# The prologue of an FFT filter and FFN kernel: zeta of batch 0 in one tile, an x load of batch 1 moved into a filter's buffer, and PSUM banks shared between two small stages

## The chip, the cores and the metric

The kernel runs on one core of one Trainium2 chip. The metric is device time in microseconds (us). A time is the median of several executions; the profile is one of them.

TensorE (PE) multiplies and writes to PSUM (eight banks). VectorE (DVE) and ScalarE (ACT) evict PSUM into SBUF. GpSimd (POOL) here only casts fp32 to fp16. SyncE (SP) issues nearly all DMA transfers, from one queue, in program order.

## The reference

```python
def _attn_ref(x, filt_r, filt_i):             # x: 8 x 3008 x 256
    X = np.fft.rfft(x, axis=1)
    Y = X * (filt_r + 1j * filt_i)[None]
    return np.fft.irfft(Y, n=x.shape[1], axis=1)

def _moe_ref(x, w_in, w_out):                 # 24064 tokens, 256 -> 2048 -> 256
    h = np.maximum(x @ w_in, 0.0)
    return h * h @ w_out
```

## The kernel before

The FFT is done by matmuls. The FFN of all 24064 tokens is the bulk of PE's work, and the transforms of batches 1 to 7 are slipped between its matmuls. Only batch 0 has nothing to hide behind: until its filtered signal is there, no FFN matmul can start. That prologue takes about 54 us, and the change concerns it alone. Its steps are: `chunk_a0` (first transform, giving uT), `turn_u` (uT turned by matmuls with the identity), `place_f` (the filter put in order by matmuls with the 0/1 matrix sPF, result sF), `unit_b` (second transform, and the product with sF on DVE), `unit_p0` (first half of the way back, giving zeta, stored to DRAM as dZ), `read_z` (dZ read back in another layout), `unit_y` (psY, the last half), and then `ffn_g1`. Batch 1's first transform (`chunk_a(1, c)`, psA) stands on PE between the last `unit_p0` and the first `unit_y`.

```python
p_x32 = pool(bufs=2)      # x in fp32, then w_in in fp32
p_ze  = pool(bufs=3)      # zeta
p_y   = pool(bufs=2)      # tag "yt": the two filters in fp32, then products, then yt
p_h2  = pool(bufs=2)      # tag "h2": several early tiles, then h of the FFN
...
def bank_pair(name):                 # rotates through the 8 PSUM banks, two at a time
    k = npair[0] % 4; npair[0] += 1
    if k < 2: t = psH(name); return [t[:, 0, :], t[:, 1, :]], [(t, 0)]
    ...                              # k == 2: two psF banks, k == 3: two psO banks
...
def unit_p0(k):
    ze = p_ze.tile([128, 6, D], F16, tag="ze", name=f"ze_0_{k}")
    ps = psH(f"psP_0_{k}")
    ...                                                           # 8 matmuls
    nc.scalar.copy(out=ze[:, 0:4, :], in_=...ps...)
    nc.sync.dma_start(out=dZ[0]...[:, 4 * k:4 * k + 4, :], in_=ze[:, 0:4, :])
...
for k in range(2): load_win(k)            # w_in into the two x32 buffers
for c in (0, 2, 1, 3): chunk_a0(c)
...                                       # POOL: filter casts, then w_in casts
for k in range(6): turn_u(k)
nc.vector.tensor_copy(...)                # last quarter of the filter casts, on DVE
for k in range(4): place_f(0, k, nc.vector if k % 2 else nc.scalar)    # psH banks only
place_f(1, 0, nc.scalar)
load_wide(1, 0); cast_wide(1, 0, nc.gpsimd, nc.gpsimd)      # x of batch 1, first third
for k in range(7):
    if k < 6:
        unit_b(0, 2 * k)
        if k < 5: place_f(1, k + 1, nc.scalar)
        unit_b(0, 2 * k + 1)
    if k > 0: unit_p0(k - 1)
    if k < 2: place_f(0, k + 4, nc.scalar)
    if k in (2, 3): load_wide(1, k - 1); cast_wide(1, k - 1, nc.gpsimd, nc.gpsimd)
    if k == 5: read_z(0, 0, (0,))         # first half of the first zt: needs stores 0 to 2
read_z(0, 0, (1,)); read_z(0, 1)
for c in (0, 2, 1): chunk_a(1, c)         # psA
...
for n in range(4): unit_y(0, n)           # psY; the FFN follows
```

## Time and profile before

| | before |
|---|---|
| time, median | 801.57 us (3 runs), 801.13 us (4 runs, with one beside the changed kernel) |
| span of the profiled run (its time: 800.30 us) | 798.5 us |
| PE busy | 782.8 us, 98% |
| granted clock, mean of the span | 0.995 |
| first psY starts | 52.84 us |

The span is the profiled execution on the core. Since PE is busy nearly always after the prologue, everything after the first psY is nearly a block of fixed length: in the profiles of this case 745.2 to 747.7 us lie behind it. So what counts first is when that block starts; the 2.5 us by which its length differs come back below. The lines that show this, and the waits in front of it, are in the prediction.

### The profile page before, as it was taken

What the parts mean: (1) busy time and instruction counts of PE and PEld (TensorE: products, weight loads), DVE (VectorE), ACT (ScalarE), POOL (GpSimd) and SP (SyncE); (2) the same over time, 40 slices, a digit from 0 to 9 for tenths busy, and PEclk for the clock granted to TensorE, in tenths of its full rate; (3) what the DMA queues carried; (4) which work ended last, traced back from release to release, by engine and by line L of the source; (5) the groups of instructions that cost most, each with busy time, mean ns of one, the idle gap of its engine ahead of it and who ended that gap; (6) DMA issues with size and microseconds to landing.
All of it is one profiled execution on the core that took longest, in us unless ns stands there. A gap on an engine that the chain in (4) does not pass through costs nothing.

```text
span 798.5 us, 14777 instructions
## 1 busy us (share of the span) xinstructions
PE 782.8 (98%) x6102; PEld 553.3 (69%) x6102; DVE 552.7 (69%) x897; ACT 554.3 (69%) x705; POOL 18.5 (2%) x23
## 2 busy tenths in 40 slices
PE   8979999999999999999999999999999999999998
PEld 5746767667676676867778676776767667676666
DVE  7847995579855897559965699556995589553342
ACT  4756776767767676777776677676777767766663
POOL 3320000000000000000000000000000000000000
PEclk9989999999999999999999999999999999999999
DMA  9886455335723467055561565525563342511111
GB/s 362 317 272 209 123 149 138 98 128 158 200 65 106 149 164 189 27 152 157 129 177 55 166 157 131 136 66 160 148 181 92 88 142 81 123 45 41 40 41 53
DMA packets 88124, 108.10 MB, mean 135 GB/s; under 512 B 6273, under 2 KB 78849, under 8 KB 83585
## 3 DMA queue, kind: packets, MB, share of 16 engines
q1 hardware_dynamic: 87848, 106.98, 46.8%
q8 instruction: 48, 0.79, 0.4%
q10 hardware_dynamic: 144, 0.18, 0.1%
q14 instruction: 20, 0.16, 0.1%
q0 software_dynamic: 64, 0.00, 0.0%
HBM read 58.90 MB, written 48.23 MB: 134 GB/s over the span
## 4 chain that ended last, share of the span: by engine, by line
PE 90%; DMA 7%; ACT 1%; DVE 1%; SPq 0%; issue 0%; ACTq 0%
PE psO L566 40%; PE psH L551 39%; PE psY L521 3%; PE psA L349 3%; PE psB L436 3%; PE psP L485 2%; DMA sPF<-cPF 2%; DMA ut<-dU 2%; DMA dZ<-ze 2%; DMA zt<-dZ 1%; PE psf L283 1%; PE psf L286 1%; ACT h L555 1%; ACT sF L293 0%; ACT ze L473 0%; DVE yt L530 0%
## 5 line engine op out<-in xcount | busy, mean ns | idle before, releaser
L555 ACT ACTIVATE h<-psH 128x1024 f16<-128x1024 f32 x376 | 384.8, 1024 | 190.3 <-PE psH L551 188.3
L566 PE MATMUL psO<-sWout,h 128*128 128x256 f16 x3008 | 388.6, 272 | 0.0
L551 PE MATMUL psH<-yt,sWin 128*128 128x512 f16 (+7 forms) x1728 | 386.9, 351 | 1.2 <-ACT h L555 0.4
L566 PEld LDWEIGHTS <-h 128*128 128x128 f16 x3008 | 290.6, 98 | 77.3
L559 DVE TENSOR_TENSOR h<-h 128x1024 f16<-128x1024 f16 x376 | 253.9, 685 | 100.7 <-ACT h L555 99.2
L551 PEld LDWEIGHTS <-sWin 128*128 128x128 f16 x1728 | 159.4, 98 | 101.1 <-issue 2.6
L444 DVE TENSOR_TENSOR prod<-psB,sF 128x1024 f16<-128x1024 f32 x84 | 102.5, 1220 | 6.4 <-PE psB L436 6.1
L530 DVE CAST yt<-psY 128x376 f16<-128x376 f32 x62 | 33.9, 549 | 57.8 <-PE psY L521 57.8
L355 DVE CAST u<-psA 96x512 f16<-96x512 f32 x50 | 34.3, 687 | 46.8 <-PE psA L349 45.1
L487 ACT CAST ze<-psP 128x512 f16<-128x512 f32 x84 | 49.2, 585 | 17.9 <-PE psP L485 16.0
L573 ACT COPY ost<-psO 128x512 f32<-128x512 f32 x94 | 55.5, 590 | 7.2 <-PE psO L566 5.8
L521 PEld LDWEIGHTS <-zt 112*128 112x128 f16 x512 | 34.8, 98 | 13.2 <-issue 3.1
L521 PE MATMUL psY<-sC,zt 112*128 112x94 f16 x512 | 42.2, 205 | 1.4 <-DMA zt<-dZ 1.0
L458 DVE TENSOR_TENSOR yf<-prod,yf 128x512 f16<-128x512 f16 x84 | 35.7, 425 | 2.9
L436 PE MATMUL psB<-ut,sSB 128*128 128x256 f16 x192 | 36.5, 272 | 0.8 <-DMA ut<-dU 0.6
L349 PE MATMUL psA<-x,sC 94*96 94x512 f16 x96 | 36.6, 382 | 0.0
L436 PEld LDWEIGHTS <-sSB 128*128 128x128 f16 x192 | 18.6, 98 | 21.4 <-issue 2.3
L485 PE MATMUL psP<-yf,sSP 128*128 128x256 f16 x168 | 32.1, 273 | 0.2 <-ACT yt L528 0.2
L528 ACT CAST yt<-psY 128x376 f16<-128x376 f32 x66 | 30.8, 468 | 1.1 <-PE psY L521 1.0
L328 DVE CAST x<-x 94x2048 f16<-94x2048 f32 x24 | 29.2, 1216 | 0.0
L353 ACT CAST u<-psA 96x512 f16<-96x512 f32 x50 | 28.6, 572 | 0.0
L451 DVE COPY yf<-prod 64x512 f16<-64x512 f16 x84 | 24.3, 289 | 2.9
(61 smaller groups left out, 248.7 us busy)
## 6 DMA issues: line engine op xcount, KB each, us to landing
x<-in_x_dram SPq DMA_DIRECT2D x20, 768.0 KB
zt<-dZ SPq DMA_DIRECT2D x64, 192.0 KB
dU<-u SPq DMA_DIRECT2D x28, 384.0 KB
dZ<-ze SPq DMA_DIRECT2D x28, 384.0 KB
out_dram<-ost SPq DMA_DIRECT2D x32, 256.0 KB
out_dram<-ost SPq DMA_DIRECT2D x64, 128.0 KB
ut<-dU SPq DMA_DIRECT2D x7, 1024.0 KB
xw<-in_x_dram SPq DMA_DIRECT2D x6, 1024.0 KB
```

Source lines behind the costliest of these rows:

```text
L349: nc.tensor.matmul(ps[0:96, :], sSA, x16s[(b, c)][:, m, :], start=True, stop=True)
L436: nc.tensor.matmul(ps[:, i * D:(i + 1) * D], sSB[:, 2 * p + i, :], uts[b][:, 2 * p + i, :], start=True, stop=True)
L444: nc.vector.tensor_mul(out=prod, in0=ps.rearrange("p (a d) -> p a d", d=D).unsqueeze(1).to_broadcast([128, 2, 2, D]), in1=sF[:, :, 2 * p:2 ...
L458: nc.vector.tensor_add(out=yf, in0=prod[:, 0], in1=yf)
L485: nc.tensor.matmul(ps[:, i * D:(i + 1) * D], sSP[:, 2 * p + i, :], yf[:, i, :], start=True, stop=True)
L487: nc.scalar.copy(out=zes[(b, c)][:, 2 * i6:2 * i6 + 2, :], in_=ps.rearrange("p (a d) -> p a d", d=D))
L521: nc.tensor.matmul(ps[:, 94 * jj:94 * jj + 94], zt[:, 4 * (g % 2) + jj, dt * 128:(dt + 1) * 128], sSY, start=True, stop=True)
L551: nc.tensor.matmul(ps[:, i, o:o + n], sWin[:, dt, jt * 128:(jt + 1) * 128], yts[b][:, dt, r:r + n], start=(dt == 0), stop=(dt == 1))
L555: nc.scalar.activation(out=h2[:, 2 * s:2 * s + 2, :], in_=ps, func=AF.Relu)
L559: nc.vector.tensor_mul(out=v, in0=v, in1=v)
L566: nc.tensor.matmul(pso[g][:, t % 2, :], h2s[g][:, jt, t * 128:(t + 1) * 128], sWout[:, jt, :], start=(jt == 0), stop=(jt == NJT - 1))
L573: nc.scalar.copy(out=ost, in_=pso[g])
```

## The change

The intent is threefold. First, zeta of batch 0 no longer rotates through three buffers but lies in one tile, so that its evictions wait for no store. Second, one x load of batch 1 goes into the buffer of the filter's real part as soon as that has been cast, ahead of the other two; load 1 is also issued one step sooner. Third, turning and placing are interleaved and rotate through all eight banks, and the last quarter of the filter casts goes from DVE to POOL.

```diff
-        pool = p_h2 if (b, k) == (0, 2) else p_x32
+        pool, tag = (p_x32, "x32") if k < 2 else (p_y, "yt") if b else (p_h2, "h2")
...
-    def place_f(im, k, eng):
-        t = psH(f"psf_{im}_{k}")
-        banks, groups = [t[:, 0, :], t[:, 1, :]], [(t, 0)]
+    def place_f(im, k, eng, rotate=False):
+        if rotate:
+            banks, groups = bank_pair(f"psf_{im}_{k}")
+        else: ...                                   # as before
...
     def unit_p0(k):
-        ze = p_ze.tile([128, 6, D], F16, tag="ze", name=f"ze_0_{k}")
+        if k == 0:
+            zes[0] = p_h2.tile([128, NC, D], F16, tag="h2", name="ze_0")
+        ze = zes[0][:, 4 * k:4 * k + 4, :]
...
-    for im, e in ((0, e0), (0, e1), (1, e0)):
+    for im, e in ((0, e0), (0, e1), (1, e0), (1, e1)):      # casts on POOL
...
+    load_wide(1, 2)
+    load_wide(1, 0)
+    for k in (2, 0):
+        cast_wide(1, k, nc.gpsimd, nc.gpsimd)
     for k in range(6):
-        turn_u(k)
-    nc.vector.tensor_copy(out=f16s[0][:, 1, e1], in_=f32s[1][:, e1])
-    for k in range(4):
-        place_f(0, k, nc.vector if k % 2 else nc.scalar)
+        turn_u(k, nc.vector if k in (1, 3, 4, 5) else nc.scalar)
+        if k > 2:
+            place_f(0, k - 3, nc.scalar, True)
+    place_f(0, 3, nc.vector, True)
     place_f(1, 0, nc.scalar)
-    load_wide(1, 0)
-    cast_wide(1, 0, nc.gpsimd, nc.gpsimd)
...
-        if k in (2, 3):
-            load_wide(1, k - 1)
-            cast_wide(1, k - 1, nc.gpsimd, nc.gpsimd)
+        if k == 1:
+            load_wide(1, 1)
+            cast_wide(1, 1, nc.gpsimd, nc.gpsimd)
```

More of the change, by code (lines that the diff above doesn't have):

```diff
@@ L217, in load_wide @@
         v1 = xrows[b * S + 2048:b * S + 3072, :].rearrange("(p m) d -> p m d", m=8)
-        pool = p_h2 if (b, k) == (0, 2) else p_x32
-        t = pool.tile([128, 8, D], F32, tag="h2" if pool is p_h2 else "x32", name=f"xw_{b}_{k}")
+        pool, tag = (p_x32, "x32") if k < 2 else (p_y, "yt") if b else (p_h2, "h2")
+        t = pool.tile([128, 8, D], F32, tag=tag, name=f"xw_{b}_{k}")
         nc.sync.dma_start(out=t, in_=(v0[:, 0:8, :], v1, v0[:, 8:16, :])[k])
@@ L269 @@
     f16s = []
-    def place_f(im, k, eng):
-        t = psH(f"psf_{im}_{k}")
-        banks, groups = [t[:, 0, :], t[:, 1, :]], [(t, 0)]
+    def place_f(im, k, eng, rotate=False):
+        if rotate:
+            banks, groups = bank_pair(f"psf_{im}_{k}")
+        else:
+            t = psH(f"psf_{im}_{k}")
+            banks, groups = [t[:, 0, :], t[:, 1, :]], [(t, 0)]
         for i in range(4):
@@ L402, in chunk_a0, with turn_u @@
                     nc.vector.tensor_copy(out=o, in_=pv)
-    def turn_u(k):
-        if k > 3:
-            npair[0] = k - 2
+    def turn_u(k, eng):
         banks, groups = bank_pair(f"psT_{k}")
@@ L412, in turn_u @@
                 nc.tensor.matmul(o, uT[:, dt, 4 * k + i, :], ident, start=True, stop=True)
-        eng = pair_engine()
         for t, i in groups:
@@ L472, in unit_p0 @@
                                  prod[:, v, i % 2, :], start=(v == 0), stop=(v == 1))
-        nc.scalar.copy(out=ze[:, 0:4, :], in_=ps.rearrange("p t (a d) -> p (t a) d", d=D))
+        nc.scalar.copy(out=ze, in_=ps.rearrange("p t (a d) -> p (t a) d", d=D))
         nc.sync.dma_start(
             out=dZ[0].rearrange("(s p) d -> p s d", p=128)[:, 4 * k:4 * k + 4, :],
-            in_=ze[:, 0:4, :])
+            in_=ze)
     def unit_p(b, p):
```

## The prediction

> **What bounds the kernel now.** I read the page first. TensorE (PE) is busy nearly throughout, so after the start-up the span is a fixed quantity of matmuls, and only the start can give time back.
>
> ```profile
> PE 782.8 (98%) x6102; PEld 553.3 (69%) x6102; DVE 552.7 (69%) x897; ACT 554.3 (69%) x705; POOL 18.5 (2%) x23
> ```
>
> Everything the diff touches lies in the first 65 us (batch 0's filter product, batch 1's first transform). So I read the chain of waits over that stretch (start us, length, what):
>
> ```profile
> 36.16 1.00 ACT ze L473
> 37.17 7.05 DMA dZ<-ze
> 44.32 1.02 ACT ze L473
> 45.36 4.06 DMA dZ<-ze
> 49.44 3.27 DMA zt<-dZ
> ```
>
> Zeta is evicted from PSUM by ScalarE (ACT) into `ze`, three buffers in rotation, stored to `dZ` and read back as `zt`. Eviction 5 needs the buffer of store 2, which was issued at 37.17 and landed only at 44.22. ACT stood still for it for 3.58 us. Then come the last store (4.06 us) and the read back (3.27 us), and only then psY, which feeds the FFN.
>
> Why did a 256 KB store take 7 us? The timeline of GpSimd (POOL) shows what else was in the queue: batch 1's x in three loads of 1 MB, cast in the order they landed.
>
> ```profile
> 31.67 2.02 POOL L310 CAST sWin<-win 128x1024 f16<-128x1024 f32 x2 [0.45 <-DMA win<-in_moe_w_in_dram]
> 36.62 2.02 POOL L227 CAST xw<-xw 128x1024 f16<-128x1024 f32 x2 [2.93 <-DMA xw<-in_x_dram]
> 43.58 2.02 POOL L227 CAST xw<-xw 128x1024 f16<-128x1024 f32 x2 [4.93 <-DMA xw<-in_x_dram]
> 46.77 2.02 POOL L227 CAST xw<-xw 128x1024 f16<-128x1024 f32 x2 [1.17 <-DMA xw<-in_x_dram]
> ```
>
> The loads reuse the buffers of w_in, so they cannot start before the POOL casts from 29.2 us on. PE waits for the second one, too, and pays twice. The windows below are 3.4 us long; columns are PE, weight load, DVE, ACT and POOL busy, granted clock, DMA share, GB/s:
>
> ```profile
> 29.20:32.70 3.50, 3.39 (x38) 2.95 (x36) 3.29 (x4) 3.24 (x4) 3.05 (x4) 1.00 0.40 89
> 39.50:42.90 3.40, 1.57 (x11) 0.93 (x10) 1.65 (x2) 1.01 (x1) 0.00 (x0) 0.99 0.97 295
> 42.90:46.30 3.40, 1.62 (x4) 0.77 (x4) 0.00 (x0) 1.16 (x2) 2.02 (x2) 0.50 1.02 367
> 46.30:49.70 3.40, 3.40 (x9) 1.62 (x8) 1.22 (x1) 1.57 (x3) 2.02 (x2) 0.50 0.52 164
> ```
>
> The DMA engines idle at 29 to 33 us (share 0.40), just before they become the bottleneck; PE is half idle at 39.5 to 42.9, and for the next 6.8 us its clock is halved.
>
> Last, the front of the stage, in PE's timeline:
>
> ```profile
> 18.32 1.16 PE L412 MATMUL psT<-sC,uT 128*128 128x128 f16 x12 [0.25 <-ACT ut L419]
> 19.69 0.38 PE L412 MATMUL psT<-sC,uT 128*128 128x128 f16 x4 [0.21 <-DVE ut L421]
> 20.57 0.28 PE L283 MATMUL psf<-f,sPF 128*128 128x256 f16 x1 [0.50 <-DMA sPF<-cPF]
> 22.73 0.27 PE L283 MATMUL psf<-f,sPF 128*128 128x256 f16 x1 [0.24 <-ACT sF L293]
> ```
>
> Turning ends at 20.07, and placing F cannot start before 20.57, because the matrix sPF lands then. Waits for PSUM banks are there, but small: 0.24 us before F(0,2), and 0.2 each before F(0,3) and F(1,0).
>
> **What the Trainium skill says.** "TensorE: Matmul & The Clock Gate", Part 1: the clock is judged in free-running windows of about 3.4 us, and after an idle one it falls to half. The trace agrees: half clock for 6.8 us, two such windows, and the 512-column matmuls then start 0.43 us apart, against 0.22 later. A window that was only about half busy (1.57 of 3.40) was enough. "DMA: Bandwidth & Descriptors", section "Anatomy of one DMA": a transfer has a fixed cost of about 2 us, mostly the wait for the written data to be confirmed. The trace fits: 256 KB at some 300 GB/s would be 0.9 us of data, yet the last store took 4.06; so store plus read back will not go away. Same page, "Queues, rings and completion order": one issuing engine has one row of rings, consumed in order. This agrees with store 2 (issued behind the second x load) landing 0.6 us after it. "Perfetto Trace Analysis", section "Matmuls": groups should rotate through PSUM banks so that evictions overlap; here that has only the waits of 0.2 us to win.
>
> **The change part by part.**
>
> 1. *All of zeta in one tile.* No eviction waits for a store any more. Product 11 on VectorE (DVE) ends at 41.14; the last four psP matmuls end at about 41.75, so ACT could start at 41.85 instead of 44.32: **-2.5 us**. The tile takes the second h2 buffer and the FFN's first h2 must wait for its stores, but psY needs them read back anyway: 0.
>
> 2. *x load 2 of batch 1 first, into the freed buffer of filter r.* POOL has read that filter by 17.86, so the load goes out right behind w_in at 21.5 and fills the idle DMA at 29 to 34: w_in ends at 31.6, and 1 MB at 420 GB/s is 2.5 us, so it lands at 34.1. Load 0 (issued at 31.24 as before) then lands at about 36.6, as before. Load 1 goes out at 33.7, when the second w_in cast ends, instead of 35.4, and lands at 40 to 41.5 instead of 43.5. The first half of its cast is ready when PE has finished psP (about 42.4), so the 2.67 us stop and the half clock behind it go. The 24 psA matmuls take 5.3 us, not 10.3, and end near 48 instead of 52.1. This is only permission: psY is set by zeta.
>
>    It also empties the queue before the last store. A megabyte less is in flight, so I take 3.0 us instead of 4.06 (estimate: a 384 KB dU store issued at 69.75 on a quiet queue landed 3.3 later): **-1.0 us**. Read back: 3.27 unchanged.
>
> 3. *Turning and placing share eight banks.* The order on PE becomes T0..T3, F0, T4, F1, T5, F2, F3. T3 ends at 18.07, and F0 still waits for sPF until 20.57. The gap grows from 0.50 to 2.50 us, and T4 and T5 (0.5 us each), which used to run before sPF came, now run after it. Against that stand the saved bank waits. By hand: F0 to 21.44, T4 to 22.0, F1 to 22.9, T5 to 23.45, F2 to 24.35, F3 to 25.25; F(1,0) still waits for the psH bank of F2, whose eviction ends at 25.57; it is ready at 26.5, and ACT starts it at 26.7 instead of 25.97: **+0.7 us**. From there ACT (1.11 per placing, 1.01 per zeta) and DVE (12 products, 1.14 apart) run nearly without gaps to 41, so the delay passes through.
>
> 4. *Last cast of filter i from DVE to POOL* (1.57 us off DVE, 1.44 on POOL, ready at about 22.9, needed at 25.6): 0.
>
> Sum without clock effects: -2.5 -1.0 +0.7 = **-2.8 us**. Last store issued at about 43.5, landed 46.5, zt at 49.8, psY 2.9 us earlier than 52.84. From 64 us on PE is the bound and the offset reaches the end.
>
> **The rivals.**
>
> *(a) The half clock comes back elsewhere.* PE now idles 2.5 us in one piece (18.07 to 20.57), and again about 2 us between psA's end (48) and zt (49.8). About 1.8 us idle in one window halved the clock in the trace. The first gap exceeds that if the window boundary does not split it; I give 60%. It would cost half a window, at most 1.7 us, say 1.3 on F(1,0), which passes through. The second, 50%, costs perhaps 1.0 at the start of the FFN, where ACT needs 1.0 us per psH against 0.87 on PE, so that some of it is hidden. Expected: 0.6 x 1.3 + 0.5 x 1.0 = **+1.3 us**. Both together would leave -0.5: about 801.
>
> *(b) x load 1 stays late.* In the kernel before it took 8 us behind the stores[...]. If it landed at 43 again, psA would end at about 49.5, still within zt's 49.8: under 0.3 us. If zeta came earlier than I say, this would become the bound.
>
> *(c) The zeta chain is not shortened*, because the last store and its read back are latency: then part 2 loses its 1.0 us, and the total is about 799.8.
>
> *(d) More is won:* if the front is not delayed (ACT's chain catches up) and the clock stays, -3.5 to -4.5, about 797.5.
>
> **Range and chances.** 801.57 - 2.8 + 1.3 = 800.1; I put the point at 799.4, a little lower, because in (a) DVE and ACT hide some of the slower PE. The three runs before spread 1.4 us. 797.0 to 801.4 should hold it 8 times in 10. Two per cent is 16 us, four times the most that rival (d) gives, so "within 2%" is nearly certain.
>
> **What would show it.** Right: no ACT wait for dZ before the sixth zeta eviction, which starts near 42.5; the first POOL cast of x at about 34; psA without a 2.7 us stop, 0.22 us apart; first psY near 50. PE idle for 2.5 us before the first psf; F(1,0) on ACT at 26 to 27. Clock 0.50 windows near 20 to 24 or near 50 to 53 show rival (a). Wrong: F placed before 20.5, psA waiting for POOL beyond 43, or psY above 52.

## More of the kernel before

Times spread by 1 to 3 us, and that spread becomes part of the story.

## The result, and the profile after

| | before | after |
|---|---|---|
| time, median (range), 4 runs each | 801.13 (800.25 to 802.06) | 797.23 (796.58 to 797.72) |
| span of the profiled run | 798.5 | 795.1 |
| first psY | 52.84 | 48.94 |

The ratio is 0.9951 (95% interval 0.9933 to 0.9968). A ratio here is the mean time of one kernel's fast runs over that of the other's of the same rounds, so it is not quite the ratio of the medians. The change is worth 0.5%, or about 3.9 us: within 2%, but clear of noise. It lies inside the predicted range (797.0 to 801.4), 2.2 us under the predicted point of 799.4.

The chain of waits of the changed kernel (start us, length, what), the stretch that answers to the one in the prediction:

```profile
41.39 0.61 PE psP L473 x4
42.03 1.02 ACT ze L475
43.07 2.61 DMA dZ<-ze
45.69 3.11 DMA zt<-dZ
...
48.94 0.33 PE psY L523 x4
```

The last zeta eviction now follows PE, not a store; it starts at 42.03 instead of 44.32. The last store takes 2.61 us instead of 4.06.

POOL's timeline of the changed kernel (start, length, line, operation, and in brackets the idle time before it):

```profile
31.59 2.03 POOL L313 CAST sWin<-win 128x1024 f16<-128x1024 f32 x2 [0.47 <-DMA win<-in_moe_w_in_dram]
34.07 2.03 POOL L227 CAST xw<-xw 128x1024 f16<-128x1024 f32 x2 [0.45 <-DMA xw<-in_x_dram]
36.83 2.03 POOL L227 CAST xw<-xw 128x1024 f16<-128x1024 f32 x2 [0.73 <-DMA xw<-in_x_dram]
40.87 2.03 POOL L227 CAST xw<-xw 128x1024 f16<-128x1024 f32 x2 [2.01 <-DMA xw<-in_x_dram]
```

The three casts of x start at 34.07, 36.83 and 40.87, where they started at 36.62, 43.58 and 46.77. The same windows as in the prediction (PE, weight load, DVE, ACT, POOL busy, granted clock, DMA share, GB/s):

```profile
29.20:32.70 3.50, 3.39 (x37) 2.95 (x36) 3.46 (x4) 3.31 (x4) 3.03 (x4) 1.00 1.10 379
39.50:42.90 3.40, 2.47 (x17) 1.49 (x15) 1.84 (x2) 1.97 (x3) 2.03 (x2) 1.00 0.91 277
42.90:46.30 3.40, 3.40 (x17) 1.92 (x16) 2.04 (x3) 2.43 (x5) 0.00 (x0) 1.00 0.47 138
46.30:49.70 3.40, 1.83 (x24) 1.28 (x23) 1.81 (x4) 1.10 (x3) 0.00 (x0) 1.00 0.82 180
```

The DMA engines are full at 29 to 33 us (before: share 0.40), PE works on psA from 41.8 at full clock, and the half-clock stretch is gone. Last, the front of the stage on PE:

```profile
17.72 1.90 PE L413 MATMUL psT<-sC,uT 128*128 128x128 f16 x31 [0.21 <-DVE uT L405]
20.45 0.28 PE L286 MATMUL psf<-f,sPF 128*128 128x256 f16 x1 [0.83 <-DMA sPF<-cPF]
21.33 0.61 PE L413 MATMUL psT<-sC,uT 128*128 128x128 f16 x8
25.26 0.28 PE L286 MATMUL psf<-f,sPF 128*128 128x256 f16 x1 [0.24 <-ACT sF L296]
```

Placing still starts when sPF lands, at 20.45, and turnings 4 and 5 now come after that. F(1,0) starts at 25.26 (before 24.88), and ACT evicts it at 26.34 (before 25.97), 0.37 us later. One thing is odd: turning ended at 19.62 here although only four of the six turnings stand before it. The reason is that the first transform began at 11.14 instead of 9.58, since the 26 warm-up matmuls took 8.63 us instead of 7.07. That is chance: the trace's record of the clock has it rise to full speed at 8.48 us here and at 5.31 in before. What follows from it is tested below.

psY is 3.90 us earlier, the span 3.4 us shorter.

### The profile page after: what moved, and what is told of

Its sections match the earlier page's. It is cut to its first block, busy times and chain, and to the rows that moved or that the text cites. A ratio compares the mean times of both kernels' runs of the same rounds, so it can differ in the third digit from the quotient of the medians.

```text
span 795.1 us, 14787 instructions
## 1 busy us (share of the span) xinstructions
PE 780.7 (98%) x6102; PEld 552.6 (69%) x6102; DVE 551.4 (69%) x897; ACT 554.3 (70%) x706; POOL 19.9 (3%) x24
## 4 chain that ended last, share of the span: by engine, by line
PE 90%; DMA 6%; ACT 1%; DVE 1%; issue 0%; SPq 0%; ACTq 0%; DVEq 0%
PE psO L568 40%; PE psH L553 38%; PE psY L523 3%; PE psB L436 3%; PE psA L352 3%; PE psP L487 2%; DMA sPF<-cPF 2%; DMA zt<-dZ 1%; DMA dZ<-ze 1%; DMA ut<-dU 1%; PE psf L286 1%; PE psf L289 1%; ACT h L557 1%; DMA dU<-u 0%; PE psP L473 0%
## 5 line engine op out<-in xcount | busy, mean ns | idle before, releaser
L358 DVE CAST u<-psA 96x512 f16<-96x512 f32 x50 | 34.3, 687 | 47.1 <-PE psA L352 45.1
L352 PE MATMUL psA<-x,sC 94*96 94x512 f16 x96 | 36.6, 382 | 0.0
```

Source lines behind the costliest of these rows:

```text
L352: nc.tensor.matmul(ps[0:96, :], sSA, x16s[(b, c)][:, m, :], start=True, stop=True)
```

## The experiments

Twelve runs were made (eleven new kernels and the changed one again), each of five rounds against the kernel before on the same chip; they fell on three chips. In the edits, "before" and "changed" name the base. All of them gave correct results. Times are in us.

| run | base and edit | median (range) | ratio to before (95% interval) |
|---|---|---|---|
| p1_zeta | before + part 1 | 800.07 (799.61 to 802.67) | 0.9996 (0.9978 to 1.0014) |
| p2_loads | before + part 2 | 799.23 (798.74 to 801.65) | 0.9985 (0.9967 to 1.0002) |
| p3_banks | before + part 3 | 800.74 (800.39 to 800.96) | 0.9998 (0.9982 to 1.0015) |
| p12_no_banks | before + parts 1 and 2 | 797.56 (797.08 to 799.71) | 0.9962 (0.9945 to 0.9979) |
| w34_no_banks | p12 with 34 warm-up matmuls | 798.80 (798.07 to 799.77) | 0.9972 (0.9955 to 0.9988) |
| w34_after | changed with 34 warm-up matmuls | 797.37 (797.05 to 798.47) | 0.9959 (0.9944 to 0.9975) |
| z_after | changed, early zt read after the last store | 796.61 (796.03 to 798.75) | 0.9950 (0.9933 to 0.9967) |
| s1_spf_after | changed, sPF loaded before the filters | 798.02 (796.08 to 798.95) | 0.9962 (0.9945 to 0.9980) |
| after_again | changed | 797.14 (797.01 to 797.90) | 0.9954 (0.9943 to 0.9966) |
| zx | z_after, x and w_in exchanged in the queue | 796.95 (796.23 to 799.55) | 0.9955 (0.9943 to 0.9968) |
| s1zx | zx, sPF loaded before the filters | 797.51 (796.95 to 798.38) | 0.9960 (0.9947 to 0.9972) |
| s1zx_warm | s1zx, eight dummy matmuls before psY | 795.35 (794.99 to 797.21) | 0.9936 (0.9923 to 0.9950) |

The kernel before gave medians of 800.26 to 801.00 beside these.

### Parts alone: the first four runs

The prediction added up parts as if each had its own gain. These runs ask whether they do.

**p1_zeta.** Edit, on the kernel before:

```diff
+        if k == 0:
+            zes[0] = p_h2.tile([128, NC, D], F16, tag="h2", name="ze_0")
+        ze = zes[0][:, 4 * k:4 * k + 4, :]
-        ze = p_ze.tile([128, 6, D], F16, tag="ze", name=f"ze_0_{k}")
```

> Kernel before with part 1 alone (zeta in one tile). Theory A, the prediction's sum (the parts add): the sixth zeta eviction starts at about 42 instead of 44.3, psY about 2.5 us earlier (50.3), time about 799. Theory B (the parts overlap; the x loads are the common cause): the eviction also starts at 42, but the last store still lands behind x loads that end at 46.7, and PE comes to psY only after psA, which still waits for x and runs at half clock until about 52.1; psY at 52.2 or later, time within 0.7 us of before.

Measured: no gain that can be told from zero. In its chain of waits:

```profile
37.18 6.48 DMA dZ<-ze
...
43.73 0.34 SPq L505
...
44.12 5.20 DMA dZ<-ze
...
49.33 3.22 DMA zt<-dZ
...
52.69 0.33 PE psY L523 x4
```

The sixth eviction did start at 41.84, just as hoped. But its store was not issued until 44.12. SP issues in order, and ahead of that store stands the read of the first half of zt (L505, issued at 43.73), which waits for store 2 (37.18, landed 43.66). So the wait for store 2 moved from ACT to SP. Then the last store needed 5.20 us behind the x loads, the last of which was cast at 46.63, and psA still ran at half clock until about 50 and ended at 52. psY came 0.15 us earlier than before. Theory A falls; B holds, with one more reason (SP's order) than it gave.

**p2_loads.** Edit, on the kernel before: the lines of the diff above that concern `load_wide`, `cast_wide` and their places; zeta stays in three buffers.

> Kernel before with part 2 alone (last x of batch 1 in a filter buffer and loaded first; zeta still in three buffers). Theory A: only the quieter queue of the last store, -1.0 us, with ACT still waiting some 2 us for a zeta store. Theory B: store 2 lands at about 42.2 (in the changed kernel the read of zt that waits for it went out at 42.25), so ACT waits under 0.5 us, the last store lands in about 2.6 us, psY near 49, time 3.5 us or so under before: nearly the whole gain.

Measured: 799.23, a gain of about 1.2 us by the ratio. The chain:

```profile
35.08 6.60 DMA dZ<-ze
...
41.78 1.02 ACT ze L473
...
43.82 3.35 DMA dZ<-ze
...
48.03 3.75 DMA zt<-dZ
```

x load 1 now goes out at 33.88, in front of store 1 (35.08), which therefore landed only at 41.68. ACT waited 2.21 us for it, before the *fifth* eviction this time. PE stood for 1.0 us behind that wait, the clock was halved from 43.4 to 46.7, psA was late, and psY came at 50.70, held last by the read of zt behind that late store. So Theory B fails: the wait for a buffer of zeta did not shrink to what was left of store 2, it moved one store forward. Theory A has the sizes right (ACT waits some 2 us for a zeta store, about 1 us is won) but did not say that it would be another store. psY is 2.14 us earlier than in before and the span only 1.3 us shorter: the last read of zt, issued at 48.03, held DVE, and with it the FFN, until 51.80.

**p12_no_banks.** Edit: both of the above.

> Parts 1 and 2 without part 3. Theory A: -3.5 us against before (part 3 cost 0.7), so a little faster than the changed kernel. Theory B: the same as part 2 alone within 0.5 us. Rival on part 3: slower than the changed kernel by up to 0.7 us.

Measured: 797.56, or about 3.0 us by the ratio. Alone, part 1 gives 0.3 us and part 2 1.2 us by their ratios (both intervals include zero); together they give twice the sum. The intervals are about 1.4 us wide to each side, so the times alone do not show that the sum is exceeded; the traces show why it should be. The parts need each other: the loads can only be moved forward without harm if zeta does not wait for the stores that they delay, and the free zeta is only of use if the last store does not stand behind loads. Theory A's statement of this kernel (a little faster than the changed one) is not borne out, nor is B's (same as part 2 alone). The rival on part 3 (slower than the changed kernel by up to 0.7 us) fits: 0.3 us at the median, 0.9 by the ratios, whose intervals overlap.

**p3_banks.** Edit, on the kernel before: the `place_f` and `turn_u` lines of the diff and the POOL cast.

> Kernel before with part 3 alone (shared banks, last filter cast on POOL). Theory A: F(1,0) on ACT 0.4 to 0.7 us later than in before when the warm-up ends early, all later events shifted by it, time +0.4 to +0.7. Rival: the order lets sPF's arrival hide the turning, so that the time is the same or a little lower, more so when the first matmuls ran at half clock for longer: 0 to -0.7. PE idle of 0.8 to 2.5 us before the first psf in either case; a halved clock after it would show in the granted clock.

Measured: the median is 0.5 us above that of before in these rounds, the ratio 0.9998. F(1,0) on ACT came at 26.43, 0.46 us later than in before, as predicted; PE idled 2.19 us in front of sPF and its clock stayed at 1.00. What is striking is the spread: 0.57 us over six runs, while before ran from 799.5 to 800.3 in six of eleven runs of these rounds and from 801.3 to 802.7 in the other five. In these six runs part 3 loses a little against the good runs and has no bad ones. The gap between good and bad runs belongs to these rounds, though: on the two other chips before ran from 799.86 to 801.83 and from 799.61 to 802.92, with runs all through the range.

### The spread: is it a late warm-up clock?

The bad runs could be those in which PE's clock rises late, as in the profiled run of the changed kernel (warm-up 8.63 us). To have that in every run, eight more warm-up matmuls were put in front:

```diff
-    for _ in range(26):
+    for _ in range(34):
```

> Parts 1 and 2 with 34 instead of 26 warm-up matmuls, so that the first transform always starts some 1.7 us later, as it did in the profiled run of the changed kernel (11.14 instead of 9.58). Theory: without part 3 all six turnings stand before the first placing, so they end near 21.7, past sPF's landing at 20.5, and the time goes to the slow group of its own runs (799.5 to 800) or 1 us over the 26 warm-ups' median of 797.6. Rival: the two groups of times come from elsewhere (DMA), and the warm-up changes nothing: 797.6.

> The changed kernel with 34 warm-up matmuls. Theory: T0 to T3 end near 19.8, still before sPF lands at 20.5, so the delay is hidden: the same as the changed kernel within 0.4 us (797.2), except in runs whose clock rises late as well (then T3 ends at about 21.3 and up to 0.8 us are lost). Rival: +1 us as in the kernel without part 3.

Measured: 798.80 without part 3 (means of six runs: 798.80 against 797.84 with 26 matmuls, so +1.0), and 797.37 with it (mean 797.60 against 797.27 in the later runs of the changed kernel, +0.3). The two ratios have overlapping intervals, and so have those of the two kernels without part 3. ACT's eviction of F(1,0), in w34_no_banks and then in w34_after:

```profile
27.68 2.38 ACT L293 ACTIVATE sF<-psf,sign 128x1024 f16<-128x1024 f32 x2 [1.14 <-PE psf L286]
```

```profile
26.23 2.21 ACT L296 ACTIVATE sF<-psf,sign 128x1024 f16<-128x1024 f32 x2 [1.14 <-PE psf L289]
```

Turning began at 18.11 and 17.65 in these two. Without part 3 the delay passes through to F(1,0) (27.68 against 25.80 in p12_no_banks); with it F(1,0) stays where it is in all profiles of the changed order with sPF loaded in its old place, at 26.2 to 26.5, because four turnings still fit in front of sPF's arrival. This is what part 3 is shown to buy: not bank waits, but a front that does not mind when the clock rises.

How much of this reaches the end is not shown. Of the 1.88 us of delay at F(1,0), 0.48 are left at psY (50.31 against 49.83), and w34_after has its psY at 50.05. Most of what the profiled w34_no_banks lost, it lost later: its first eviction of the FFN (h from psH, on ACT) is 0.47 us behind that of p12_no_banks (53.37 against 52.90), its last one 1.85 us (786.23 against 784.38). Between 100 and 790 us PE waited for the second transform's input, which is read back from DRAM (total us, times, longest), in w34_no_banks and then in p12_no_banks:

```profile
PE psB L436 <- DMA ut<-dU: 1.7, 4, 0.8
PE psB L436 <- DMA ut<-dU: 0.5, 1, 0.5
```

So in this profile DMA waits far behind the prologue weigh more than the front, which is what the expectation's rival had in mind. Another candidate is the half clock: four of the five slow runs of before in these rounds have a mean clock of 0.995 or 0.996, five of the six fast ones 0.997 or 0.998 (but in p3_banks runs with 0.995 and with 0.998 take the same time). A late rise of the clock does not show in that mean (the changed kernel's profile, with its late rise, has 0.999). That the slow runs of before are those with a late clock therefore stays open; no profile of before caught one.

### What is left: moving the next limits

**z_after.** Edit, on the changed kernel:

```diff
-        if k == 5:
-            read_z(0, 0, (0,))
-    read_z(0, 0, (1,))
+    read_z(0, 0)
```

> The changed kernel, the read of the first half of zt put behind the last zeta store in SyncE's queue. Theory: the last store no longer stands behind a wait for store 2; it had 0.0 us (changed kernel's profile) to 0.8 us (without part 3) of that, and the second half of zt now has one more transfer ahead of it (about 0.4 us): -0.3 to +0.3. Rival: the early half read matters, +0.5 or more.

Measured: 796.61, 0.5 to 0.6 under the changed kernel's medians; the ratio's interval overlaps with it, so this is not settled; the expected range was -0.3 to +0.3. In the profile the last store took 2.34 us instead of 2.61; the DMA engines stood idle when it began (share 0.00 from 43.5 to 44.0), and the read of zt was issued 0.5 us behind it.

**s1_spf_after.** sPF gates the front in all profiles. It is only 192 KB, so here it goes before the filters:

```diff
-    load_f(0)
-    load_f(1)
     nc.sync.dma_start(out=sPF, in_=...)
+    load_f(0)
+    load_f(1)
```

> The changed kernel with the sPF load issued before the two filter loads. Theory A (sPF gates the front): placing starts when T3 ends (18.1 to 19.6) instead of 20.5; F(1,0) on ACT at 24.3 to 25 instead of 26.3, the zeta chain 1.4 to 2 us earlier. Theory B: the gain is not seen at the end, because x load 1 still lands at about 41 and psA stands before psY on PE (psA cannot end before 47.2), and because the last store stands in SyncE's queue behind a wait for store 2 (about 42.2): psY at 48.5 to 49, time within 0.5 us of the changed kernel.

Measured: 798.02, *slower* than the changed kernel by 0.8 at the median (796.08 to 798.95, and the ratios' intervals overlap; the profile is of the slowest run). The front did move: F(1,0) on ACT at 24.87, the sixth zeta eviction at 40.56. But PE now came to psA 1.5 us sooner, and x load 1 did not:

```profile
43.08 0.59 PE L373 MATMUL psA<-xw,sC 120*96 120x512 f16 x1 [2.33 <-POOL xw L227]
43.45 0.63 PE L371 MATMUL psA<-xw,sC 128*96 128x512 f16 x1
43.88 0.63 PE L373 MATMUL psA<-xw,sC 120*96 120x512 f16 x1
```

PE waited 2.33 us and its clock fell to half at about 41.8, for two windows: the psA matmuls start 0.43 us apart. psY came at 50.82, nearly 2 us later than in the changed kernel. In this profile an earlier front turned into a later end. Theory B is right on where the gain goes, but it had no loss in it.

**after_again, zx, s1zx.** The changed kernel again, and two kernels on z_after in which x loads 0 and 1 take w_in's place in the queue (and its buffers) and w_in theirs:

```diff
-    for k in range(2):
-        load_win(k)
+    load_wide(1, 0)
+    load_wide(1, 1)
...                                  # w_in: loads where x loads 0 and 1 were, casts behind the loop
```

> The changed kernel once more, for the runs beside it and for the spread: median 797.2, most runs within 796.6 to 797.7. Theory on the clock: a run with a mean granted clock of 0.998 (one window of 3.4 us at half clock is 0.5 x 3.4 / 798 = 0.002) is 1 to 2 us slower than those at 1.0; about one run in six.

> The changed kernel with the early zt read behind the last store, and with batch 1's x loads 0 and 1 in the queue places and buffers of w_in and w_in in theirs. Theory: x is all landed by 34, so psA no longer depends on it, but in the changed kernel psA was not waiting for x any more and psY is set by zeta: the same as with the moved read alone (796.6) within 0.4 us. Rival: x's arrival still costs; then 1 us or more under 797.2.

> As zx, and sPF loaded before the filters. Theory: with sPF first alone, the front came 1.5 us earlier, but PE then waited for x load 1 at 42 and its clock was halved for psA, which gave all back and more. With x there, psA runs from 40.4 to 45.7 at full clock, the last store goes out at 41.6, and psY comes at about 47.5 to 47.8: 1 to 1.5 us under the changed kernel, about 795.8. Rival: psA was not the cause, and the time stays near 797.9. Risk: PE then idles 2 us before psY, so some runs may lose a window of clock there.

Measured: the changed kernel repeats at 797.14; none of its five runs had a clock of 0.998, so the slow one in six did not appear. zx is at 796.95, as expected not better than z_after: psA was hardly waiting for x any more. s1zx fails its expectation, 797.51 instead of 795.8, though its psY came at 48.31, 0.6 us before the changed kernel's. Its windows from 46 us on tell why (columns as above):

```profile
46.00:49.30 3.30, 1.36 (x26) 1.11 (x24) 1.43 (x3) 0.58 (x3) 0.00 (x0) 1.00 0.93 207
49.30:52.70 3.40, 3.12 (x12) 1.07 (x9) 0.78 (x2) 1.40 (x2) 0.00 (x0) 0.52 1.03 308
```

PE had 1.94 us of nothing to do between psA and psY, and the FFN began at half clock (0.52). All five runs have a mean granted clock of 0.995 to 0.998, where those of the changed kernel have 0.999 or 1.0.

**s1zx_warm.** Edit, on s1zx, in `unit_y`:

```diff
+        if n == 0 and b == 0:
+            for _ in range(8):
+                nc.tensor.matmul(ps, zero, sF[:, 0, 0:2, :], start=True, stop=True)
```

> As s1zx, with eight 512-column matmuls of a zero matrix into psY's bank between psA and psY (1.7 us of the 2.2 us in which PE had nothing to do). Theory: in s1zx psY came 0.6 us earlier than in the changed kernel, but PE's clock was halved from 49.3 to 52.6 after its idle time, and all five runs showed 0.995 to 0.998; with PE kept busy the clock stays, the granted clock is 0.999 to 1.0 in most runs, and the time is 1.3 to 2 us under s1zx's 797.5: about 795.8, under the changed kernel. Rival: the half clock hid behind ACT and DVE, and the time stays at 797.3 or so.

Measured: 795.35, with the granted clock at 0.999 or 1.0 in five of six runs. The same windows:

```profile
46.00:49.30 3.30, 3.17 (x33) 1.97 (x32) 1.57 (x4) 0.78 (x2) 0.00 (x0) 1.00 0.95 197
49.30:52.70 3.40, 2.89 (x12) 1.16 (x12) 1.22 (x3) 2.09 (x3) 0.00 (x0) 1.00 1.09 315
```

Eight useless matmuls in a gap were worth 2.2 us at the median (797.51 to 795.35; not the same rounds nor the same chip, but the same kernel of before beside each), and 1.9 us by the ratios to it, 0.9960 and 0.9936. This version has the lowest median of all, 1.8 us under the changed kernel's; by the ratios (0.9936 against 0.9951 and 0.9954) it is 1.2 to 1.4 us, with intervals that just overlap.

The clock also fits the outliers of other kernels, none of which was profiled. One window of 3.4 us at half clock lowers the mean by 0.5 x 3.4 / 798 = 0.002. The slowest run of p12_no_banks (799.71), of z_after (798.75), of zx (799.55) and of w34_after (798.47) each has a clock of 0.998, 1.1 to 2.6 us above the median of its kernel. The slowest run of w34_no_banks (799.77) has a clock of 1.0; it is the one with the DMA waits shown above.

## Why the prediction was right or wrong

The time lies in the range, and the main steps came as told. The terms, with psY as the yardstick (52.84 to 48.94, -3.90):

1. **Zeta evictions, -2.5.** In the sum the sixth one is 2.29 us earlier with 0.37 of delay from the front in it, so -2.66: right in size. Wrong in attribution: "*All of zeta in one tile* ... **-2.5 us**" was told as part 1's own gain. p1_zeta shows that part 1 alone is worth nothing at the end, since the wait for store 2 passes to SP's queue and the last store to its place behind the x loads. The prediction had rival waits for other parts, and none for this one.
2. **Loads, "permission" and -1.0 on the last store.** The arrivals were right (34.07, 36.83 and 40.87 against 34.1, 36.6 and 40 to 41.5), psA ran at full clock without a stop (41.83 to 47.1). The last store fell by 1.45 us (4.06 to 2.61), in after_again by 0.93 (3.13). The term was right within its scatter. Not foreseen was that moving the loads alone gains only about 1.2 us as long as zeta is not free as well: in p2_loads the loads moved forward made a zeta buffer wait of their own (2.21 us).
3. **Shared banks, +0.7.** Measured +0.37 on F(1,0) here, +0.46 in p3_banks; the mechanism (a longer gap before sPF, two turnings after it) was right and the size half. But this term looked only at one profile. The profiles show that the order makes the front independent of the time at which the clock rises (F(1,0)). Whether it costs anything in the *mean* of runs is not settled: the changed kernel's means are 797.19 and 797.27, that of p12_no_banks 797.84, and one run of 799.71 makes more than half of that difference. An earlier front is in part lost in SP's queue as well: in p12_no_banks the sixth eviction ended at 42.67, but its store went out at 43.42, behind the zt read at 42.99, which waits for store 2.
4. **Rival (a), +1.3 for the clock.** This is the step that failed: an expected cost of 1.3 us, and none came. None of the nine runs of the changed kernel has a granted clock under 0.999, and in after_again PE idled 2.23 us in front of the first psf with the clock at 1.00. The rule drawn from one window ("about 1.8 us idle in one window halved the clock") came with a condition, "if the window boundary does not split it", and in both profiles that had the first gap in full, after_again and p3_banks, a boundary did fall into it (the last section lays the windows out). In the profiled run of the changed kernel the gap was only 0.83 us, by the chance of the late warm-up. The second gap escaped narrowly: its window had PE busy for 1.85 us in the changed kernel and for 1.69 us in after_again, where 1.68 us in p2_loads were followed by half clock. But the term makes up less of the miss between 799.4 and 797.2 than its size suggests, because the point had already taken 0.7 of the 1.3 back. What is left: 0.6 of clock, 1.1 of parts (psY at -3.90 instead of -2.8: the last store 0.45, the front 0.33, zeta and the read back 0.16 each), and 0.4 because the kernel before itself ran at 801.13 and not 801.57. Yet the fear was not empty: with the front moved by 1 to 1.5 us, the clock did fall (s1_spf_after, s1zx), at a cost of about 2 us.
5. **Rival (b)** did not bind in the changed kernel, but only just: the first psA matmuls waited 0.21 us for POOL in after_again, and 0.7 us in w34_after. The prediction's remark that it "would become the bound" if zeta came earlier is what s1_spf_after shows.

From psY on the offset reaches the end almost whole: -3.90 at psY, -3.4 in the span and -3.9 in the medians. This does not hold to better than about 1 us from profile to profile, as p2_loads and w34_no_banks show.

## What to carry to other kernels

A wait that you remove is only gone if nothing behind the same event is waiting as well: here one slow store was awaited by ACT's buffer, by SP's queue and, through the shared DMA engines, by the last store, and two changes that measured 0.3 and 1.2 us alone (neither clear of zero) measured 3 together. Let a stage that does not depend on a late transfer run in front of it in program order, but no more of it than fits. And count PE's idle gaps in a short stage by the clock that follows, not by their own length alone; here eight matmuls of zeros were cheaper than an empty gap. Before you give a spread of 1 us to the stage that you changed, compare the profiles at its end and at the end of the kernel.

## What the Trainium skill lacked or had wrong

- "TensorE: Matmul & The Clock Gate", Part 1, has the clock fall after an idle window of about 3.4 us. Here a window that was idle for about half of it was enough. The traces' record of the clock changes at whole multiples of 3.413 us (before: 5.31, 42.86, 49.68), so the windows can be laid out from the first rise. Full-speed windows that half clock followed had PE busy for 1.42 us (p1_zeta, 39.85 to 43.26) to 1.68 us (p2_loads, 40.00 to 43.41); in windows that it did not follow, PE was busy for 1.59 us (w34_after, 46.70 to 50.11), 1.69 (after_again, 46.50 to 49.92) or more. These overlap, so PE's busy time (its ends are modelled) does not give the exact threshold. The gap of 2.23 us in after_again, 18.17 to 20.40, was cut by a boundary at 19.20, with PE busy for 2.13 and 2.21 us in the two windows; in p3_banks the boundary was at 19.56, with 2.00 and 2.43. The page's remark that the warm-up varies from run to run agrees: the same 26 matmuls took 7.07, 7.37 and 8.63 us.
- "DMA: Bandwidth & Descriptors", section "Anatomy of one DMA", fits 2.0 us plus bytes / 436 GB/s, but to transfers issued from GpSimd; it gives no such fit for SyncE, which issues all stores here. For 256 KB the fit would be 2.6 us, an estimate from the page's figures. The last store took 2.34 (z_after), 2.61 (changed) and 3.13 us (after_again) once x had landed; zeta stores took 4.06, 5.20 and 7.05 us with loads of 1 MB in flight, which such a fit leaves out.
- The same section says that the issuing sequencer waits on semaphores before dispatch. It does not go on to what that costs a transfer behind the waiting one: in p1_zeta a store ready at 42.85 went out at 44.12, because a read that was not ready stood before it.
